# Sums of squares for the weight bounds, 512 and 64 columns down, and products on VectorE in a fused attention and gated block

## The chip, the cores and the metric

The kernel runs on one core of a Trainium2 chip. The metric is the device time of one execution in microseconds (us). Engines are named as the profile names them: PE is TensorE's matmul, PEld its weight load, DVE is VectorE, ACT ScalarE, POOL GpSimd, and SP the engine whose queue issues the DMAs.

## The reference

For x of 2048 rows and 576 columns, normalized to xn (mean and variance over the columns):

```
xn = layernorm(x)
q, k, v = split(xn @ wqkv)                 # 32 heads of 18
s = softmax(q k^T / sqrt(18), causal, window of 256 keys) v, heads joined, @ wo
h = (xn @ w_gate) * (xn @ w_up)            # 4608 hidden columns, no nonlinearity
g = silu(h @ w_down)
out = x + s * g
```

All inputs and the output are float32. Every product of two float32 matrices is made on PE from float16 halves: a high part and a low part, in three passes (high with high, high with low, low with high).

## The kernel before, in words

**Prologue (about 180 us).** The rows are normalized and transposed into `XT`, v is made for all rows and q and k are made and written to DRAM. Meanwhile the first weights and sums for the gated part are prepared at hand-set places.

**Slots.** The gated part works in 72 slots: 18 groups of 256 hidden columns, and in each group four chunks (c0 to c3) of 512 rows. A slot has 16 places. `seven_place` (L1110) issues 96 matmuls of 256 columns in a slot, spread over the places by `SEVEN_N`: seven units `q`, in the order 0, 2, 1, 3, 4, 5, 6, which together make gate and up by a scheme with seven instead of eight block products, from weights (`upw`), sums of weight blocks (`tw`) and sums of x blocks (`sx`). At place 11 `seven_half` (L1066, L1068) adds four matmuls that use 64 rows. A unit's result is read by `seven_copy` (ACT, L1078) or `seven_add` (DVE, L1082) into `gt`, and a following unit accumulates in the same PSUM bank; there are two such `up` banks. `seven_mult` (L1088) multiplies gate by up, 256 columns at a time, into `ht`: four products a slot, those of units 1, 4 and 5 on POOL and that of unit 6 on DVE. `h_hi` (ACT, L968) and `h_lo` (DVE, L973) split `ht` into the halves `hh`.

**Down.** `down` (L986) multiplies a slot's `hh` by the down weights `dnw` in the slot that follows: eight runs of six matmuls of 288 columns (four row blocks, two halves of the 576 columns). Each run fills the single `dn` PSUM bank, and DVE adds it, times a scale, into `acc` in SBUF (L991; L989 in the first group). The last six slots use the four `s` banks instead.

**Attention.** In slots 1 to 64 one step s of attention (two heads, 512 queries) lies in each slot. For each of four query blocks i and two heads j: `score_pairs` (PE, L867, two blocks at a time, 54 rows, the two heads in two row halves of the array), `score` (DVE, L877: adds the mask, takes the maximum, writes `sm_`), `shifted` (ACT, L885), `probs` (ACT: exponential L889, copy to float16 `pp` L892), `turn_probs` (POOL, L898: the low part by a subtraction; after the second head SP issues a DMA that transposes `pp` into `pt`, L901), `weigh` (PE, L910, 37 columns). `finish` (DVE, L921 to L925) divides by the row sums, `finish2` (POOL) splits, and the output goes to DRAM. `load_k`, `load_q`, `load_v` are DMAs for the step that follows.

**Weights.** For each group, one group ahead: `ffn_raw` loads gate, up and down weights (one buffer of each kind); `ffn_amax` (DVE, L410) takes the largest absolute value of each half, six reductions a group; `ffn_spread_out` sends these bounds to DRAM and `ffn_spread_in` loads them into all partitions; `ffn_scale` makes scales that are powers of two; `up_hi`, `t_hi`, `dn_hi` (ACT, L181) and `up_lo`, `t_lo`, `dn_lo` (DVE, L184) split the scaled weights; `t_sum` (POOL, L476) makes the sums of weight blocks; `dn_low` (POOL, L573) makes a third form of the down weights.

**What sets the order.** The program is a list written out by hand: `at(slot, place, f, ...)` puts f at a place (places over 15 run on into the slots that follow), and table `AT` holds the places: for a group counted from the start of the group before it, for a step of attention from the start of its slot. At a place the matmuls of `seven_place` come first, then the list's entries, `score_pairs` ahead of `down` ahead of the rest. Each engine works through its own instructions in that order, and SP its DMAs.

Of the kernel before, what the change touches and what calls it, by code (L numbers as in the profile page):

```python
# [20 lines left out]
def kernel(  # L21
# [46 lines left out]
    AT = {"amax": (13, 16, 22, 24, 6, 10),  # L68
           "dn": ((43, 46), (48, 49), (52, 54)),
           "down": (7, 9, 11, 13, 15, 17, 19, 22),  # L70
           "end": (28, 29, 33),
           "g0": (-21, -19, -13, -18, -14, -12, -11, -9),
           "h": ((16, 18), (18, 21)),
           "load": (0, 12, 12),
           "mult": {1: 2, 4: 1, 5: 1, 6: 0},
# [6 lines left out]
           "pairs": (3, 12),  # L82
           "raw": (6, 8, 13, 15, -3, -3),
           "scale": (25, 31, 38),
           "sum": ((32, 36, 46, 61, 61), (40, 48, 48, 62, 62)),
# [5 lines left out]
           "t_hi": ((57, 58), (62, 62)),  # L91
           "t_lo": ((57, 60), (64, 65)),
           "u0": ((-6, -4, -4, -3), (-5, -2, 4, -3)),
           "up_hi": (40, 44, 61, 69),
           "up_lo": (42, 44, 64, 71)}
# [309 lines left out]
    def ffn_amax(g, kind, half):  # L405
        if (g, "am") not in SC:
            SC[g, "am"] = ring.tile([128, 2, 3], F32, name="am", bufs=2)
        r = RAW[g, kind]
        r = r[:, half] if kind == 2 else r[:, :, half * 128:(half + 1) * 128]
        nc.vector.tensor_reduce(SC[g, "am"][:, half, kind:kind + 1], r, axis=AX.X if kind == 2 else AX.XY,  # L410
                                op=OP.max, apply_absolute_value=True)

    def first_bound(kind):

        if kind == 0:
            SC[0, "am"] = ring.tile([128, 2, 3], F32, name="am", bufs=2)
            nc.gpsimd.memset(SC[0, "am"], 0.0)
        am = SC[0, "am"]
        if kind < 2:
            square(am[:, 0, kind:kind + 1], RAW[0, kind].rearrange("p k n -> p (k n)"),  # L420
                   rv.rearrange("p k n -> p (k n)").bitcast(BF))
        else:
            nc.scalar.activation(am[:, 0, 0:2], am[:, 0, 0:2], AF.Sqrt)

    def ffn_spread_out(g):
        am = SC.pop((g, "am"))
        both = ring.tile([128, 3], F32, name="both", bufs=1)
        nc.vector.tensor_reduce(both, am.rearrange("p h k -> p k h"), axis=AX.X, op=OP.max)
        spread_out(f"f{g}", both, 3)
# [10 lines left out]
    def ffn_scale(g):  # L440
        sc = SC[g] = ring.tile([128, 12], F32, name="sc", bufs=3)
        nc.vector.tensor_reduce(sc[:, 0:3], SC.pop((g, "sp")), axis=AX.X, op=OP.max)
        power(sc[:, 0:3], sc[:, 3:6], sc[:, 6:9], FTOP)
        nc.gpsimd.tensor_tensor(sc[:, 9:10], sc[:, 3:4], sc[:, 4:5], op=OP.mult)
        nc.gpsimd.tensor_scalar(sc[:, 9:10], sc[:, 9:10], C_FFN, None, op0=OP.mult)
        nc.gpsimd.tensor_tensor(sc[:, 9:10], sc[:, 9:10], sc[:, 5:6], op=OP.mult)

    def up_hi(g, k):
        w = UW[g, k] = up_ring()
        hi(w[:, 0:5], RAW[g, k % 2][:, :, k // 2 * 128:k // 2 * 128 + 128], SC[g][:, 6 + k % 2:7 + k % 2])  # L450
# [120 lines left out]
    def dn_low(g, k):  # L571
        w = DW[g, k]
        nc.gpsimd.tensor_scalar(w[:, 2], w[:, 0], 1.0 / LO, None, op0=OP.mult)  # L573
# [32 lines left out]
    for k in range(3):  # L606
        at(0, AT["g0"][k], first_bound, k)
    for half in range(2):
        at(0, AT["g0"][3 + half], ffn_amax, 0, 2, half)
    for k, f in enumerate((ffn_spread_out, ffn_spread_in, ffn_scale)):  # L610
# [216 lines left out]
    QS, KS, VT, SP, SM, PP, PT, PVB, OB, O3, MX = {}, {}, {}, {}, {}, {}, {}, {}, {}, {}, {}  # L827
# [42 lines left out]
    def score(s, j, i):  # L870
        ps = SP.pop((s, j, i))
        n = (i + 3 - max(first_kb(s), i)) * 128
        sm = att.tile([128, 384], F32, name="sm_", bufs=4)
        if j == 0:
            MX[s, i] = att.tile([128, 2, 2], F32, name="mx", bufs=3)
        mx = MX[s, i][:, :, j]
# [403 lines left out]
```

## Time and profile before

| | |
|---|---|
| median of 3 runs | 1661.95 us (1661.13 to 1664.15) |
| the profiled execution | 1662.5 us, of which span (first to last instruction) 1660.8 us |
| granted TensorE clock | 1.0 |
| PE, DVE, ACT, POOL busy | 1599.0, 1387.8, 1029.3, 966.8 us |

The page's row of a group reads: line, engine, operation, what it writes and reads, shape, count, then busy time and the mean of one in ns, then the idle time of the engine ahead of these and what ended it. A row of waits reads: who waited for whom, total us, times, the longest. A row of the windows view gives a stretch, its length, and for each engine the busy time (with the count of instructions), then clock, DMA share and GB/s. In a timeline the first number is the start, the second the duration, and x6 stands for six merged instructions. Busy times count overlapping instructions once; the durations of neighbours on one engine overlap a little, so the distance between starts is the shorter measure of cost.

### The profile page before, as it was taken

Reading aid. Unit: us, or ns where it says so; the run is one execution under the profiler, and the core shown is the slowest. Engines: PE = TensorE matmul, PEld = TensorE weight load, DVE = VectorE, ACT = ScalarE, POOL = GpSimd, SP = SyncE. Lnnn points to the kernel's source line nnn. Section 1 sums busy time; section 2 is a strip of 40 time slices with the busy share of each in tenths; the row PEclk is TensorE's granted clock in tenths of the full one; section 3 lists DMA queues with packets and bytes.
Section 4 is the critical chain, followed back from the end, with each engine's and each line's share of the span. In section 5 each row is a group of like instructions: output and inputs, shape, how many; then the busy total and the mean of one; then the engine's idle time right before and its main releaser. Section 6 shows DMA issues by size and latency. Waiting matters only on the chain.

```text
span 1660.8 us, 40615 instructions
## 1 busy us (share of the span) xinstructions
PE 1599.0 (96%) x15498; PEld 1232.4 (74%) x15498; DVE 1387.8 (84%) x3136; ACT 1029.3 (62%) x1934; POOL 966.8 (58%) x1209
## 2 busy tenths in 40 slices
PE   8999899999999999999999999999999999999999
PEld 5464577877877777777777777777777777778787
DVE  7537789889898989898989898989898989987655
ACT  6434476767676777767776676777767776743230
POOL 3124675757575767676766767676767685843100
PEclk9999999999999999999999999999999999999999
DMA  9562346565656777767677677768776867651228
GB/s 233 164 183 100 111 81 129 94 125 97 124 108 118 136 124 130 124 131 123 136 118 141 119 144 110 146 111 150 108 148 107 153 106 150 118 102 34 63 65 221
DMA packets 565748, 206.95 MB, mean 125 GB/s; under 512 B 506288, under 2 KB 546352, under 8 KB 565552
## 3 DMA queue, kind: packets, MB, share of 16 engines
q1 hardware_dynamic: 565552, 204.35, 63.0%
q8 instruction: 121, 1.98, 0.5%
q14 instruction: 75, 0.61, 0.1%
HBM read 76.63 MB, written 23.75 MB: 60 GB/s over the span
## 4 chain that ended last, share of the span: by engine, by line
PE 59%; DVE 30%; DMA 5%; issue 3%; POOL 1%; ACT 1%; SPq 0%; DVEq 0%; POOLq 0%; ACTq 0%
PE up L1110 25%; PE dn L986 16%; DVE acc L991 5%; DVE gt L1082 4%; DVE upw L184 4%; DVE hh L973 4%; PE s L372 3%; DMA pt<-pp 3%; DVE tw L184 3%; PE pv L910 2%; PE s L986 2%; PE s L1217 2%; DVE ht L1088 2%; PE s L867 1%; PE up L1217 1%
## 5 line engine op out<-in xcount | busy, mean ns | idle before, releaser
L986 PE MATMUL dn<-dnw,hh 128*128 128x288 f16 x3168 | 475.1, 286 | 26.0 <-DVE acc L991 22.1
L986 PEld LDWEIGHTS <-hh 128*128 128x128 f16 x3456 | 328.1, 98 | 150.3 <-issue 81.6
L1110 PEld LDWEIGHTS <-tw 128*128 128x128 f16 x3456 | 317.6, 97 | 63.6 <-issue 23.6
L1110 PEld LDWEIGHTS <-upw 128*128 128x128 f16 x3456 | 327.9, 98 | 45.4 <-DVE gt L1082 1.8
L1110 PE MATMUL up<-XT,upw 128*128 128x256 f16 x2304 | 329.8, 272 | 1.0 <-DVE gt L1082 0.9
L991 DVE SCALAR_TENSOR_TENSOR acc<-dn,sc,acc 128x288 f32<-128x288 f32 x496 | 253.3, 511 | 90.5 <-PE dn L986 87.0
L885 ACT ACTIVATE mx<-mx,sig 128x2 f32<-128x2 f32 x256 | 98.3, 384 | 308.2 <-DVE mx L877 308.0
L1088 POOL TENSOR_TENSOR ht<-gt 128x256 f32<-128x256 f32 x216 | 158.3, 733 | 207.9 <-ACT gt L1078 127.3
L1082 DVE SCALAR_TENSOR_TENSOR gt<-up,gt 128x512 f32<-128x512 f32 x360 | 246.0, 683 | 39.4 <-PE up L1110 22.1
L1110 PE MATMUL up<-XT,tw 128*128 128x256 f16 x1728 | 245.9, 272 | 10.3 <-DVE gt L1082 10.3
L1110 PE MATMUL up<-sx,tw 128*128 128x256 f16 x1728 | 223.6, 272 | 0.3 <-ACT gt L1078 0.3
L910 PEld LDWEIGHTS <-pt 128*128 128x128 f16 x2880 | 118.4, 96 | 20.1 <-DMA pt<-pp 9.9
L910 PE MATMUL pv<-vt,pt 128*128 128x37 f16 x2880 | 123.0, 179 | 6.5 <-DMA pt<-pp 6.4
L973 DVE SCALAR_TENSOR_TENSOR hh<-hh,ht 128x512 f16<-128x512 f16 x144 | 128.5, 893 | 0.0
L1078 ACT ACTIVATE gt<-up 128x512 f32<-128x512 f32 x144 | 84.9, 590 | 63.3 <-PE up L1110 62.0
L1110 PE MATMUL up<-sx,upw 128*128 128x256 f16 x864 | 117.7, 273 | 1.5 <-DVE gt L1082 1.5
L968 ACT ACTIVATE hh<-ht 128x512 f16<-128x512 f32 x144 | 89.3, 620 | 47.0 <-POOL ht L1088 46.9
L184 DVE SCALAR_TENSOR_TENSOR upw<-raw,sc,upw 128x640 f16<-128x640 f32 x72 | 95.6, 1329 | 0.0
L476 POOL TENSOR_TENSOR tf<-raw 128x256 f32<-128x256 f32 x102 | 91.4, 896 | 1.3
L410 DVE TENSOR_REDUCE am<-raw 128x1 f32<-128x640 f32 (+1 forms) x104 | 81.7, 786 | 0.0
L181 ACT ACTIVATE upw<-raw,sc 128x640 f16<-128x640 f32 x72 | 58.7, 817 | 15.6 <-DVE sc L160 10.4
L867 PE MATMUL s<-ks,qs 54*128 54x384 f16 (+2 forms) x512 | 63.7, 317 | 2.9 <-DMA qs<-qk_d 2.7
(2310 smaller groups left out, 2854.6 us busy)
## 6 DMA issues: line engine op xcount, KB each, us to landing
raw<-in_B_w_down_dram SPq DMA_DIRECT2D x36, 288.0 KB
qk_d<-qp SPq DMA_DIRECT2D x18, 512.0 KB
raw<-in_B_w_gate_dram SPq DMA_DIRECT2D x36, 256.0 KB
raw<-in_B_w_up_dram SPq DMA_DIRECT2D x36, 256.0 KB
vt<-v_d SPq DMA_DIRECT2D x48, 111.0 KB
ks<-qk_d SPq DMA_DIRECT2D x96, 54.0 KB
v_d<-vo SPq DMA_DIRECT2D x16, 296.0 KB
xr<-in_A_x_dram SPq DMA_DIRECT2D x16, 288.0 KB
```

The costliest lines, as they stand in the source:

```text
L184: nc.vector.scalar_tensor_tensor(w, rv, s, h, op0=OP.mult, op1=OP.subtract)
L476: nc.gpsimd.tensor_tensor(t[:, to], x0, x1, op=OP.subtract)
L885: nc.scalar.activation(mx[:, 1], mx[:, 0], AF.Identity, bias=sig[:, 2:3], scale=sig[:, 1:2])
L910: nc.tensor.matmul(PVB[s][:, j, i, :VW], pt[:, 2 * nb * j + n], VT[s][:, lo_ + n % nb, j * VW:(j + 1) * VW], start=n == 0, stop=n == 2 * n ...
L968: nc.scalar.activation(hh[:, 0], h, AF.Copy, scale=1.0 / LO)
L973: nc.vector.scalar_tensor_tensor(hh[:, 1], hh[:, 0], -LO, h, op0=OP.mult, op1=OP.add)
L986: nc.tensor.matmul(ps[:, :HALF], a, b, start=q == 0, stop=q == len(l) - 1)
L991: nc.vector.scalar_tensor_tensor(d, ps[:, :HALF], SC[g][:, 9:10], d, op0=OP.mult, op1=OP.add)
L1078: nc.scalar.activation(seven_new(sl, name), CH[q], AF.Copy, scale=H_SC)
L1082: nc.vector.scalar_tensor_tensor(seven_new(sl, name), CH[q], H_SC, x, op0=OP.mult, op1=OP.add)
L1088: eng.tensor_tensor(HT[sl, f][:, 256 * i:256 * i + 256], u[:, 0:256], u[:, 256:512], op=OP.mult)
L1110: nc.tensor.matmul(CH[q][:, o], a, b, start=CH["first"], stop=last and q != 4, skip_group_check=q in ON)
```

## The change

1. **Bounds.** `ffn_amax` is one ACT square with a sum for each kind (128 x 1280 for gate and up, 128 x 1152 for down) instead of two DVE reductions; its output goes to a `upw` buffer that is allocated earlier for it. `ffn_scale` takes a root by halving the exponent (two small DVE operations more); three small POOL operations move to `ffn_scale2` at a later place. The reduction over halves in `ffn_spread_out` goes.
2. **Down.** Four runs of six matmuls of 512 columns, one for each row block, and a fifth run of 24 matmuls of 64 columns that does all four row blocks' last columns in one bank; five DVE evictions of 512, 512, 512, 512 and 256 elements.
3. **Products.** All four of `seven_mult` on DVE, that of unit 4 five places behind its unit.
4. **Second scores** at place 11 instead of 12, right behind the half passes; the first at place 4 instead of 3.
5. **Probabilities.** The two heads share a tile `sm_` (two buffers of 768 instead of four of 384), and after both exponentials one ACT copy of up to 768 elements replaces two; `pp` holds both high parts, then both low parts.
6. **Finish** multiplies by the reciprocal in PSUM (288 elements) ahead of the additions instead of after them (144).
7. **Places.** New values in table `AT`, for the prologue's sums and their engines too. `dn_low`, `finish2` and the subtractions get a switch for another engine that is off.

```diff
-    AT = {"amax": (13, 16, 22, 24, 6, 10),
+    AT = {"amax": (15, 20, 11),
+           "eng": (1, 1, 1, 1, 0, 0, 0, 0, 0, 0, 0, 0, 0, 0),
-           "dn": ((43, 46), (48, 49), (52, 54)),
+           "dn": ((42, 42), (48, 54), (52, 56)),
-           "down": (7, 9, 11, 13, 15, 17, 19, 22),
+           "down": (7, 10, 13, 16, 20),
-           "h": ((16, 18), (18, 21)),
+           "h": ((15, 18), (18, 21)),
-           "load": (0, 12, 12),
+           "load": (0, 8, 10),
-           "mult": {1: 2, 4: 1, 5: 1, 6: 0},
+           "mult": {1: 1, 4: 5, 5: 1, 6: 1},
-           "pairs": (3, 12),
+           "pairs": (4, 11),
-           "raw": (6, 8, 13, 15, -3, -3),
+           "raw": (4, 8, 13, 15, -1, 0),
-           "scale": (25, 31, 38),
+           "scale": (23, 31, 35, 48),
-           "up_hi": (40, 44, 61, 69),
+           "up_hi": (42, 36, 63, 69),
...
-    def ffn_amax(g, kind, half):
...
-        nc.vector.tensor_reduce(SC[g, "am"][:, half, kind:kind + 1], r, axis=AX.X if kind == 2 else AX.XY,
-                                op=OP.max, apply_absolute_value=True)
+    def ffn_amax(g, kind):
...
+        am, r = SC[g, "am"], RAW[g, kind].rearrange("p k n -> p (k n)")
+        to = rv if g == 0 else UW[g, 0]
+        square(am[:, kind:kind + 1], r, to.rearrange("p k n -> p (k n)").bitcast(BF))
...
     def probs(s, j, i):
         sm, mx, n = SM[s, j, i]
         nc.scalar.activation(sm, sm, AF.Exp, bias=mx[:, 1:2], scale=sig[:, 0:1])
-        if j == 0:
+        if j == 1:
             PP[s, i] = att.tile([128, 1536], F16, name="pp", bufs=3)
-        nc.scalar.copy(PP[s, i][:, 2 * n * j:2 * n * j + n], sm)
+            nc.scalar.copy(PP[s, i][:, 0:2 * n].rearrange("p (j n) -> p j n", j=2), SMT.pop((s, i))[:, :, 384 - n:])
...
+        nc.vector.tensor_tensor(pv[:, :, :, 0:2 * DH], pv[:, :, :, 0:2 * DH], rc.to_broadcast([128, 2, 4, 2 * DH]),
+                                op=OP.mult)
...
-        nc.vector.tensor_tensor(o3, o3, rc.to_broadcast([128, 2, 4, DH]), op=OP.mult)
...
     def down(sl, n):
...
+        cols = slice(0, 512) if n < 4 else slice(512, D)
+        for i in (n,) if n < 4 else range(4):
+            to = ps if n < 4 else ps[:, 64 * i:64 * i + 64]
...
+        d, src = acc[:, 4 * c + n, cols] if n < 4 else acc[:, 4 * c:4 * c + 4, cols], ps
+        if n == 4:
+            src = ps[:, 0:256].rearrange("p (i n) -> p i n", i=4)
...
-            at(sl, place + AT["mult"][4], seven_mult, sl, "v", 1, 1, gp)
+            at(sl, place + AT["mult"][4], seven_mult, sl, "v", 1, 1, (gp, vec)[AT["eng"][1]])
```

More of the change, by code (lines that the diff above doesn't have):

```diff
@@ L403, in ffn_raw @@
             nc.sync.dma_start(r[:, part], w_down[g * 256 + part * 128:g * 256 + (part + 1) * 128])
-    def ffn_amax(g, kind, half):
[L406 to L410, printed above, removed]
-                                op=OP.max, apply_absolute_value=True)
[L413 to L423, printed above, removed]
+    def ffn_amax(g, kind):
+        if kind == 2:
+            SC[g, "am"] = ring.tile([128, 3], F32, name="am", bufs=2)
+            if g:
+                UW[g, 0] = up_ring()
+        am, r = SC[g, "am"], RAW[g, kind].rearrange("p k n -> p (k n)")
+        to = rv if g == 0 else UW[g, 0]
+        square(am[:, kind:kind + 1], r, to.rearrange("p k n -> p (k n)").bitcast(BF))
     def ffn_spread_out(g):
[L426 to L429, printed above, removed]
+        spread_out(f"f{g}", SC.pop((g, "am")), 3)
     def ffn_spread_in(g):
@@ L448, in up_hi @@
     def up_hi(g, k):
-        w = UW[g, k] = up_ring()
+        if (g, k) not in UW:
+            UW[g, k] = up_ring()
+        w = UW[g, k]
         hi(w[:, 0:5], RAW[g, k % 2][:, :, k // 2 * 128:k // 2 * 128 + 128], SC[g][:, 6 + k % 2:7 + k % 2])
@@ L606 @@
     for k in range(3):
[L607 to L610, printed above, removed]
+        at(0, AT["g0"][k], ffn_amax, 0, (2, 0, 1)[k])
+    for k, f in enumerate((ffn_spread_out, ffn_spread_in, ffn_scale, ffn_scale2)):
         at(0, AT["g0"][5 + k], f, 0)
@@ L933, in finish2 @@
         oh, ol = (ob[:, k, :, f].rearrange("p i (j d) -> p i j d", j=2) for k in range(2))
-        nc.gpsimd.tensor_copy(oh, ov)
+        if AT["eng"][5]:
+            nc.scalar.copy(oh, ov)
+        else:
+            nc.gpsimd.tensor_copy(oh, ov)
         nc.gpsimd.tensor_tensor(ol, ov, oh, op=OP.subtract)
@@ L1003 @@
                 at(b, max(AT["raw"][2 * kind + part], part if g == 1 else -16), ffn_raw, g, kind, part)
-            for half in range(2):
-                at(b, AT["amax"][2 * kind + half], ffn_amax, g, kind, half)
-        for f, p in zip((ffn_spread_out, ffn_spread_in, ffn_scale), AT["scale"]):
+            at(b, AT["amax"][kind], ffn_amax, g, kind)
+        for f, p in zip((ffn_spread_out, ffn_spread_in, ffn_scale, ffn_scale2), AT["scale"]):
             at(b, p, f, g)
@@ L1021 @@
             at(sl, (17, 18)[ft] if last else AT["h"][1][ft], h_lo, sl, ft)
-        for n in range(8):
-            at(sl + 1, ((6, 7, 8, 9, 10, 11, 13, 15) if last else AT["down"])[n], down, sl, n)
+        for n in range(5):
+            at(sl + 1, ((5, 7, 9, 11, 13) if last else AT["down"])[n], down, sl, n)
     CH = {}
@@ L1131, in seven_read @@
             seven_copy(sl, 1, "11")
[L1132 removed]
+            at(sl, place + AT["mult"][1], seven_mult, sl, "11", 0, 0, (gp, vec)[AT["eng"][0]])
         elif q == 3:
```

60 lines of the change are left out of this document (33 added, 27 removed), and 22 rows, old and new, of the table AT.

## The prediction

> **What bounds the kernel now.** I read the page first, for the engines' shares:
>
> ```profile
> span 1660.8 us, 40615 instructions
> PE 1599.0 (96%) x15498; PEld 1232.4 (74%) x15498; DVE 1387.8 (84%) x3136; ACT 1029.3 (62%) x1934; POOL 966.8 (58%) x1209
> PE 59%; DVE 30%; DMA 5%; issue 3%; POOL 1%; ACT 1%; SPq 0%; DVEq 0%; POOLq 0%; ACTq 0%
> ```
>
> PE looks full, yet 30% of the chain that ended last runs over DVE. So I cut one group of four slots (10) out of the steady part and set a late slot without attention beside it, in the windows view:
>
> ```profile
> core 0: us, PE busy (x) PEld busy (x) DVE busy (x) ACT busy (x) POOL busy (x), PEclk, DMA share, GB/s
> 967.50:988.20 20.70, 19.57 (x205) 15.41 (x204) 20.67 (x44) 14.28 (x27) 12.06 (x16) 1.00 0.80 164
> 988.20:1008.30 20.10, 19.26 (x206) 15.31 (x205) 16.64 (x43) 13.27 (x27) 10.73 (x14) 1.00 0.77 133
> 1008.30:1028.00 19.70, 19.48 (x207) 15.42 (x206) 16.71 (x42) 15.13 (x29) 13.62 (x19) 1.00 0.68 111
> 1028.00:1048.40 20.40, 19.64 (x207) 15.48 (x205) 18.93 (x41) 14.50 (x28) 19.18 (x21) 1.00 0.65 107
> 1539.30:1556.10 16.80, 16.80 (x151) 14.14 (x149) 11.57 (x22) 2.34 (x4) 2.38 (x4) 1.00 0.02 1
> 179.90:199.50 19.60, 11.83 (x102) 9.42 (x101) 17.23 (x23) 6.16 (x11) 17.71 (x16) 1.00 0.42 123
> 253.90:483.60 229.70, 225.48 (x2306) 181.00 (x2304) 203.58 (x499) 156.43 (x318) 146.84 (x202) 1.00 0.59 110
> 562.60:1450.00 887.40, 856.28 (x8979) 677.43 (x8977) 803.16 (x1827) 629.11 (x1167) 611.33 (x738) 1.00 0.72 129
> ```
>
> I call the four slots of a group c0 to c3. In c0 DVE is busy 20.67 of 20.70 us: it is the bound. In c3 it has 1.47 us free, while POOL is busy 19.18 of 20.40. In c1 and c2 DVE has 3 us free. The last row holds 44 slots, 20.17 us each, 80.7 a group.
>
> What would PE alone need? Its timeline in c2 gives the start of each run of matmuls:
>
> ```profile
> 1019.25 0.90 PE L986 MATMUL dn<-dnw,hh 128*128 128x288 f16 x6
> 1019.98 0.93 PE L1110 MATMUL up<-sx,tw 128*128 128x256 f16 x7
> 1020.74 0.38 PE L1110 MATMUL up<-XT,upw 128*128 128x256 f16 x2
> 1021.06 0.28 PE L1066 MATMUL up<-XT,upw 64*128 64x256 f16 x1
> ...
> 1021.18 0.27 PE L1066 MATMUL up<-XT,upw 64*128 64x256 f16 x1
> ...
> 1021.38 0.91 PE L986 MATMUL dn<-dnw,hh 128*128 128x288 f16 x6
> 1022.13 0.46 PE L910 MATMUL pv<-vt,pt 128*128 128x37 f16 x12
> 1022.43 0.93 PE L1110 MATMUL up<-XT,tw 128*128 128x256 f16 x7
> 1023.29 0.50 PE L867 MATMUL s<-ks,qs 54*128 54x384 f16 x4
> 1023.72 0.72 PE L1110 MATMUL up<-XT,tw 128*128 128x256 f16 x5
> ```
>
> From start to start, six down matmuls of 288 columns take 0.73 us (0.122 each, 0.42 ns a column) and seven of 256 take 0.76 (0.109 each). Two of 256 ahead of the half passes take 0.32, 0.10 more than 0.22: going from 128 to 64 rows costs 0.10. The second pair of half passes needs 0.20 where the first needed 0.12: 0.08 to go back. The scores, in 54 rows, show the same: 0.86 for seven ahead of them (0.10 over), 0.43 for two pairs of 384 columns at 0.16 (0.11 over). A slot has three such excursions. PE's floor is the late slot's 16.80, two score excursions (0.52 each with the way in) and 48 pv matmuls at 0.025: 19.0 us. What lies above it, 1.1 us a slot, is waiting.
>
> **The change, part by part.** Durations by operation, from the groups:
>
> ```profile
> L991 DVE SCALAR_TENSOR_TENSOR acc<-dn,sc,acc 128x288 f32<-128x288 f32 x496 | 253.3, 511 | 90.5 <-PE dn L986 87.0
> L1088 POOL TENSOR_TENSOR ht<-gt 128x256 f32<-128x256 f32 x216 | 158.3, 733 | 207.9 <-ACT gt L1078 127.3 <-DVE gt L1082 80.3
> L1088 DVE TENSOR_TENSOR ht<-gt 128x256 f32<-128x256 f32 x72 | 52.2, 726 | 0.0
> L410 DVE TENSOR_REDUCE am<-raw 128x1 f32<-128x640 f32 x68 | 55.1, 810 | 0.0
> L300 ACT ACTIVATE rv<-raw 128x1280 bf16<-128x1280 f32 x2 | 2.6, 1278 | 1.9 <-POOL am L417 1.9
> L892 ACT CAST pp<-sm__2242 x1: 511/511/511, 214.4 to 214.4; 128x384 f16<-128x384 f32 x1
> L898 POOL TENSOR_TENSOR pp<-sm__2242,pp x1: 924/924/924, 215.0 to 215.0; 128x384 f16<-128x384 f32 x1
> ```
>
> *Scores behind the half passes.* The second score excursion joins that of the half passes: one way in and one way out go, 0.19 us a slot.
>
> *Down by 512 and 64 columns.* 48 matmuls of 0.122 are 5.86 us. After: 24 of 512 columns at 0.42 ns (0.217) and 24 of 64 at 0.027, 5.86 again. The cover is that a weight load hides behind matmuls even of 37 columns: twelve pv took 0.30 us, loads included. I take 0. On DVE eight evictions become five. DVE's timeline, here at the start of c0, shows what instructions cost from start to start:
>
> ```profile
> 967.54 0.68 DVE L1082 SCALAR_TENSOR_TENSOR gt<-up,gt 128x512 f32<-128x512 f32 x1
> 968.14 0.50 DVE L991 SCALAR_TENSOR_TENSOR acc<-dn,sc,acc 128x288 f32<-128x288 f32 x1
> 968.57 0.89 DVE L1088 TENSOR_TENSOR ht<-gt 128x256 f32<-128x256 f32 x1
> 969.38 1.53 DVE L184 SCALAR_TENSOR_TENSOR upw<-raw,sc,upw 128x640 f16<-128x640 f32 x1
> 970.84 0.74 DVE L184 SCALAR_TENSOR_TENSOR tw<-tf,sc,tw 128x512 f16<-128x512 f32 x1
> 971.50 0.51 DVE L991 SCALAR_TENSOR_TENSOR acc<-dn,sc,acc 128x288 f32<-128x288 f32 x1
> ```
>
> An eviction of 288 takes 0.43. One of 512 lies between 0.60 (L1082) and 0.66 (L184, which like it takes its scale from a column): 0.66. Of 256: about 0.40. So 4 x 0.66 + 0.40 = 3.04 for 3.44: -0.40 a slot. PE's one down bank is asked for every third place or later, not every second: an eviction may come about a place (1.2 us) later before PE feels it.
>
> *Bounds on ACT.* DVE loses, at 0.07 less than the duration (0.81 for 640 elements; by the elements 0.73 for the down weights' 576), 2 x 0.66 + 0.74 = 2.06 us in c0 and 3 x 0.74 = 2.2 in c1. ACT gains two squares of 1.28 and one near 1.2, 3.7 us a group, and gives back four of eight 0.51 copies a slot for a wider one: a copy of 768 lies between 0.51 and 1.02; with 0.17 us for 224 elements more (L991 to L1082 on DVE, 0.51 to 0.68) I take 0.83, -0.7 us a slot. ACT has 5 us a slot free; a square can hold one gt copy back by 1.3 us, and q1, which waits for it, comes only after q2. I take 0, up to 0.5 a group. Two small DVE operations on three columns more and one fewer, and `ffn_scale2` later on POOL: 0. The scale itself moves from place 38 to 35, the load of the spread bounds stays at 31: if DVE stood for all three places it cost 3.6 us a group; since the q and v loads no longer stand right ahead of that load on SP, I take 0 to 0.5.
>
> *Three products to DVE.* This is the term that decides. On DVE the product depends on what POOL does. Two rows, of late slots with little POOL work and of c3; c0 had 0.89, above:
>
> ```profile
> L1088 DVE TENSOR_TENSOR ht<-gt 128x256 f32<-128x256 f32 x3 | 1.2, 416 | 0.0
> L1088 DVE TENSOR_TENSOR ht<-gt 128x256 f32<-128x256 f32 x1 | 1.2, 1184 | 0.0
> ```
>
> Bounds 0.34 and 1.10 us from start to start. The mean, 0.726, gives 0.65; POOL loses three products (2.2 us) a slot, so it collides less: 0.62, three times 1.86 us a slot. The same relief of DVE's other operations with two SBUF inputs (0 to -0.4) I leave out. [...]
>
> *Finish* multiplies 288 elements in PSUM instead of 144 in SBUF: between -0.4 (the one that goes has two SBUF inputs and can collide like a product) and +0.43 (an eviction of 288, were the old one free) a slot; nearer to neither, I take 0.
>
> *The sum.* DVE, start to start: c0 20.67 - 0.40 - 2.06 + 1.86 = 20.07; c1 15.9; c2 18.17; c3 18.93 - 0.40 + 1.86 = 20.39. PE's floor is now 18.85. So c1 and c2 go to PE: 19.05 and 19.2 with small waits. c3 and c0, back to back, are DVE's: 40.46, 0.5 for the waits of its own that stay, less the 1.2 that PE now bears: 39.75. The group is 78.0 after 80.7, and 0.5 goes to new stalls (below): -2.2, 12 groups, -26 us. The twelve earlier slots (229.7 us, shorter scores, 19.14 each): 0.19 and some 0.3 of waits, -6. The prologue's reordered steps end in the first slot, 179.90 to 199.50, where PE is busy 11.83 of 19.60 us and DVE and POOL work off the sums: three bounds go and three products come there, so I take 0, with up to 7.8 to win and as much to lose. The other first slots -1; the end, where DVE has 5 us a slot free, 0. Together -33 us: the profiled execution took 1662.5 (span 1660.8, 1.7 around it), 0.5 over the median, so 1629.
>
> **Rivals.** PE's waits in the steady 44 slots:
>
> ```profile
> PE dn L986 <- DVE acc L991: 17.3, 43, 1.1
> PE pv L910 <- DMA pt<-pp: 6.4, 9, 1.2
> ```
>
> *DVE's lateness never reaches PE.* For it: the down bank, most of the waits, gets slack. All slots near 18.95: 48 x 1.2 + 12 x 0.7 = -66, some 1597.
>
> *The products are dear.* At 0.9 us each, c0 and c3 gain 0.84 again, c2 0.5: the 2.2 are eaten, and 1655 stays. For it: the products of c0 and c3 shown above. Against: those products stood where POOL had a subtraction each time. From about 0.95 on there is no gain; at 1.10 it is 1670.
>
> *Transposes come too late (slower).* Before, the first copy and subtraction (L892, L898) lay ahead of or beside the second exponential; now two exponentials, one copy and both subtractions follow each other ahead of a transpose: 0.83 for 2 x 0.51, and one subtraction of 0.92 more, 0.7 us later, 256 times. Besides, four q loads and the v load move on SP from place 12 to 8 and 10, past the transposes of places 9 and 12, which stand behind them if SP is late. Against: pv waited for a transpose 9 times in 44 slots, so most have slack; the up weights' loads, which follow the transpose of place 12, get out sooner, and so does the next transpose; POOL is freer. It decides from one transpose in six late in full (43 x 0.75 = 32); with one in three it is 1692.
>
> *The 64-column matmuls wait for their weights (slower).* A load's own row:
>
> ```profile
> L986 PEld LDWEIGHTS <-hh 128*128 128x128 f16 x3456 | 328.1, 98 | 150.3 <-issue 81.6 <-DVE hh L973 0.6
> ```
>
> At 0.098 a pair instead of 0.027, 24 x 0.07 x 72 = +122: 1751. The pv rows, 0.025 a pair, speak against it. [...]
>
> **How the numbers follow.** The forecast, 1629 (1612 to 1648), has 0.55; PE's floor (1597) 0.12; dear products (1650 to 1670) 0.18, of which 0.08 faster, 0.05 within 0.2%, 0.05 slower; late transposes 0.12; weights 0.03. Measurement tells 0.2%, 3.3 us. So faster 0.75, same 0.05, slower 0.20. The range 1600 to 1664 leaves out the two slower mechanisms and part of the floor case.
>
> **What would show it.** Right: c0 and c3 shorten to about 19.9, c1 and c2 to about 19.1; PE's waits for L991's successor fall below 10 us; the DVE product's mean is 0.6 to 0.7; the half passes run straight into scores; down of 64 at 0.027. Wrong: a product mean above 0.9 with c3 over 20.7; PE waiting on pt<-pp over 30 us; 64-column pairs near 0.1; DVE waiting for the spread bounds, whose use moves from seven to four places behind their load.

## The result, and the profile after

The changed kernel takes 1653.93 us (median of 20 runs, 1647.09 to 1662.78), the kernel before on the same chips 1663.34 (20 runs, 1658.35 to 1668.92). The ratio is 0.9944, 95% interval 0.9929 to 0.9959: 9.4 us less, where 33 were forecast. The profiled execution after took 1657.39 us, 3.5 over its median; the readings below are its own, against the 1660.8 us span of before.

The page: the span, the engines' shares and the chain that ended last.

```profile
span 1655.5 us, 40444 instructions
PE 1584.0 (96%) x15498; PEld 1122.7 (68%) x15498; DVE 1353.2 (82%) x3049; ACT 1042.3 (63%) x1781; POOL 784.0 (47%) x993
PE 56%; DVE 23%; DMA 8%; issue 4%; SPq 4%; POOL 3%; ACT 1%; DVEq 0%; ACTq 0%; POOLq 0%
```

DVE's part of the chain fell from 30% to 23%, but DMA and SP's queue, together 5% before, now hold 12%. Something that DMAs set has come into the path. Where it sits shows in the windows view of the changed kernel: the same group (10) as before, slot by slot, then slot 70, the twelve early slots, and the same 44 steady slots that the prediction cut out.

```profile
958.80:978.00 19.20, 19.02 (x207) 13.89 (x206) 18.42 (x44) 16.20 (x28) 9.85 (x13) 1.00 0.87 163
978.00:998.50 20.50, 19.02 (x206) 13.80 (x204) 14.20 (x37) 14.31 (x25) 7.91 (x10) 1.00 0.93 141
998.50:1019.00 20.50, 19.19 (x206) 13.79 (x205) 18.21 (x43) 14.79 (x25) 11.90 (x15) 1.00 0.64 121
1019.00:1038.30 19.30, 19.07 (x207) 13.92 (x206) 18.97 (x41) 12.55 (x22) 15.36 (x18) 1.00 0.55 109
1546.30:1570.70 24.40, 18.69 (x151) 13.09 (x149) 13.50 (x26) 5.33 (x9) 0.19 (x1) 0.86 0.43 100
251.30:485.20 233.90, 224.78 (x2307) 163.05 (x2305) 200.58 (x484) 157.65 (x289) 116.07 (x166) 0.99 0.59 108
562.00:1439.60 877.60, 842.46 (x8978) 610.02 (x8977) 771.08 (x1772) 635.61 (x1057) 497.16 (x606) 1.00 0.75 130
```

The DVE-bound slots c0 and c3 went down, to 19.20 and 19.30, and DVE is no longer full in c0. But c1 and c2, which had DVE to spare, went up, to 20.50. The 44 steady slots gained 9.8 us (887.4 to 877.6), the early ones lost 4.2 (229.7 to 233.9), and slot 70 takes 24.40 us for the work of a late slot that the prediction set at 16.80.

Over all runs of this study the same figure, the mean slot of the twelve steady groups (slots 16 to 63, worked out from the start of each slot's first up matmul), tells most:

| kernel | c0 | c1 | c2 | c3 | group | slot 70 |
|---|---|---|---|---|---|---|
| before | 20.73 | 19.76 | 19.62 | 20.41 | 80.5 | 20.8 |
| after | 19.13 | 20.62 | 20.57 | 19.23 | 79.5 | 24.4 |
| up loads later | 19.14 | 18.94 | 21.34 | 19.23 | 78.7 | 25.8 |
| two copies | 20.24 | 19.08 | 19.99 | 19.18 | 78.5 | 25.1 |
| scale alone at 38 | 19.17 | 20.17 | 21.84 | 19.24 | 80.4 | 24.7 |
| scale and its POOL part at 35 | 19.10 | 20.28 | 19.84 | 18.90 | 78.1 | 24.9 |
| the same at 38 | 19.07 | 20.17 | 19.85 | 18.88 | 78.0 | 25.3 |
| products on POOL | 21.30 | 20.99 | 20.63 | 19.17 | 82.1 | 24.0 |
| before, down by 512 | 20.00 | 21.27 | 19.41 | 19.78 | 80.5 | 23.0 |
| the same, up loads later | 20.07 | 19.53 | 19.71 | 19.74 | 79.1 | 22.5 |
| loads, scale and wo_scale | 19.22 | 19.05 | 20.81 | 18.87 | 78.0 | 16.8 |
| copies, scale and wo_scale | 20.25 | 19.36 | 19.17 | 19.00 | 77.8 | 16.8 |
| loads, copies, scale and wo_scale | 20.33 | 18.87 | 20.64 | 18.88 | 78.7 | 16.8 |
| wo_scale alone later | 19.18 | 20.61 | 20.62 | 19.23 | 79.6 | 16.8 |

Who waits on PE now? Its largest waits after:

```profile
PE pv L908 <- DMA pt<-pp: 24.1, 20, 2.6
PE up L1116 <- DVE gt L1088: 11.8, 7, 5.7
PE dn L991 <- DVE acc L998: 10.6, 25, 0.9
PE dn L991 <- DVE hh L975: 9.5, 12, 0.8
```

The wait that the change was to relieve, for the down bank, halved (10.6 us after, 22.1 in the whole span before). The one for transposes went from 6.4 to 24.1 us.

**The place in c1.** SP's timeline of the changed kernel around the start of c1 (978.0), and then PE's row at the place that waits:

```profile
978.84 0.78 SPq L177 DMA_DIRECT2D raw<-in_B_w_up_dram  x1
...
980.86 0.48 SPq L179 DMA_DIRECT2D raw<-in_B_w_up_dram  x1
981.51 1.96 SPq L899 DMA_TRANSPOSE pt<-pp  x1
```

```profile
987.25 0.47 PE L908 MATMUL pv<-vt,pt 128*128 128x37 f16 x12 [1.48 <-DMA pt<-pp]
```

The third transpose of the step stands on SP behind four issues of raw up weights (2.5 us). It goes out 3.5 us into c1. PE goes on 5.7 us later, after standing for 1.48. Over the twelve steady groups this transpose goes out 4.1 us into c1 (the median of the SP rows), where before it was 3.3.

**The place in c2.** DVE's timeline after, at place 35, where `ffn_scale` now lies, shows three of its small dependent operations; then POOL's shows what ran beside them.

```profile
1004.53 0.77 DVE L433 TENSOR_SCALAR sc<-sc 128x3 f32<-128x3 f32 x1
1005.33 0.84 DVE L157 TENSOR_SCALAR sc<-sc 128x3 f32<-128x3 f32 x1
1006.20 0.65 DVE L159 TENSOR_SCALAR sc<-sc 128x3 int32<-128x3 int32 x1
```

```profile
1004.35 1.79 POOL L896 TENSOR_TENSOR pp<-sm__15722,pp 128x384 f16<-128x384 f32 x2 [2.76 <-ACT pp L890]
1006.11 0.72 POOL L472 TENSOR_TENSOR tf<-raw 128x256 f32<-128x256 f32 x1
```

Three columns took 0.65 to 0.84 us an operation, where each of the same kind took 0.17 before (L156, L158 and L160, 0.169 to 0.172 in all 18 groups). The whole chain lasts 3.9 us, and the eviction and `hh` behind it come late: in this slot PE waits 0.51 for L998 and 0.80 for L975. Before, POOL did not run there, because it stood at the scale's own POOL part, right behind; POOL's waits before have this row:

```profile
POOL sc L444 <- DVE sc L158: 68.2, 18, 8.5
```

**The clock.** The windows view after, cut at the clock's steps: a stretch of 3.4 us with a wait in it, and the one that follows it; then another wait, after which the clock stayed.

```profile
258.20:261.60 3.40, 1.50 (x24) 1.13 (x23) 2.59 (x11) 2.85 (x8) 0.79 (x1) 1.00 0.49 124
261.60:265.00 3.40, 3.40 (x13) 1.50 (x11) 0.42 (x1) 3.13 (x6) 1.98 (x4) 0.50 1.13 224
...
1224.20:1227.60 3.40, 1.71 (x23) 1.38 (x24) 1.38 (x5) 3.37 (x7) 0.00 (x0) 1.00 0.60 94
```

PE at a granted clock of 0.50 does 13 matmuls in 3.4 us, six of them of 512 columns at 0.43 us instead of 0.215. After has 24.0 us of half clock in all, 3.5 of them in the tail; before has 3.3, all in the tail. So some 20 us ran at half speed: at most about 10 us lost, an estimate that takes PE as the bound in all of it.

### The profile page after: what moved, and what is told of

It reads as the page before. It is cut to its first block, busy times and chain, and to the rows that moved or that the text cites. A ratio compares the mean times of both kernels' runs of the same rounds, so it can differ in the third digit from the quotient of the medians.

```text
span 1655.5 us, 40444 instructions
## 1 busy us (share of the span) xinstructions
PE 1584.0 (96%) x15498; PEld 1122.7 (68%) x15498; DVE 1353.2 (82%) x3049; ACT 1042.3 (63%) x1781; POOL 784.0 (47%) x993
## 4 chain that ended last, share of the span: by engine, by line
PE 56%; DVE 23%; DMA 8%; issue 4%; SPq 4%; POOL 3%; ACT 1%; DVEq 0%; ACTq 0%; POOLq 0%
PE up L1116 23%; PE dn L991 14%; DMA pt<-pp 6%; PE s L373 3%; DVE gt L1088 3%; PE pv L908 3%; DVE acc L998 3%; DVE ht L1094 2%; DVE upw L185 2%; PE s L991 2%; DVE hh L975 2%; PE s L1223 2%; PE s L864 1%; PE up L1223 1%; PE up L373 1%
## 5 line engine op out<-in xcount | busy, mean ns | idle before, releaser
L991 PE MATMUL dn<-dnw,hh 128*128 128x512 f16 (+1 forms) x3168 | 448.9, 287 | 21.4 <-DVE acc L998 10.6
L1116 PEld LDWEIGHTS <-tw 128*128 128x128 f16 x3456 | 329.5, 98 | 78.0 <-issue 13.3
L991 PEld LDWEIGHTS <-hh 128*128 128x128 f16 x3456 | 224.6, 98 | 198.8 <-issue 37.6
L998 DVE SCALAR_TENSOR_TENSOR acc<-dn,sc,acc 128x512 f32<-128x512 f32 x310 | 214.7, 693 | 115.5 <-PE dn L991 110.2
L908 PE MATMUL pv<-vt,pt 128*128 128x37 f16 x2880 | 123.8, 179 | 24.3 <-DMA pt<-pp 24.1
L1094 DVE TENSOR_TENSOR ht<-gt 128x256 f32<-128x256 f32 x288 | 147.0, 530 | 0.0
L975 DVE SCALAR_TENSOR_TENSOR hh<-hh,ht 128x512 f16<-128x512 f16 x144 | 102.4, 711 | 0.1
L472 POOL TENSOR_TENSOR tf<-raw 128x256 f32<-128x256 f32 x102 | 74.2, 735 | 6.9 <-DVE sc L430 6.8
L301 ACT ACTIVATE upw<-raw 128x1280 bf16<-128x1280 f32 (+1 forms) x51 | 62.7, 1230 | 14.4 <-DMA raw<-in_B_w_up_dram 14.1
L185 DVE SCALAR_TENSOR_TENSOR upw<-raw,sc,upw 128x640 f16<-128x640 f32 x72 | 69.7, 969 | 0.0
L472 POOL TENSOR_TENSOR tf<-raw,tf 128x256 f32<-128x256 f32 x68 | 49.7, 731 | 35.3 <-DVE tw L185 35.3
```

The costliest lines, as they stand in the source:

```text
L185: nc.vector.scalar_tensor_tensor(w, rv, s, h, op0=OP.mult, op1=OP.subtract)
L472: nc.gpsimd.tensor_tensor(t[:, to], x0, x1, op=OP.subtract)
L908: nc.tensor.matmul(PVB[s][:, j, i, :VW], pt[:, nb * j + n + n // nb * nb], VT[s][:, lo_ + n % nb, j * VW:(j + 1) * VW], start=n == 0, stop ...
L975: nc.vector.scalar_tensor_tensor(hh[:, 1], hh[:, 0], -LO, h, op0=OP.mult, op1=OP.add)
L991: nc.tensor.matmul(to, a, b, start=q == 0, stop=q == len(l) - 1)
L998: nc.vector.scalar_tensor_tensor(d, src, SC[g][:, 9:10], d, op0=OP.mult, op1=OP.add)
```

## The experiments

Unless it is said otherwise, each kernel is the changed one with the edit shown. Times are medians, ratios are to the kernel before.

### The transposes of c1: loads later, and the two copies back

```diff
-    AT = {"amax": (15, 20, 11),
+    AT = {"amax": (15, 25, 11),
-           "raw": (4, 8, 13, 15, -1, 0),
-           "scale": (23, 31, 35, 48),
+           "raw": (4, 8, 17, 17, -1, 0),
+           "scale": (27, 31, 35, 48),
```

> The changed kernel with the loads of the up weights moved from places 13 and 15 to 17, behind the transpose of place 16 on SP (their bound from 20 to 25, its way out from 23 to 27). Theory A: c1 stands (20.6 us on average, with 0.8 to 2.6 us of waiting at place 6) because the third transpose of a step leaves SP behind four weight loads, and its data behind theirs: then c1 falls to about 19.0 and the time by 15 to 20 us, to about 1636. Rival B: the transpose is late because of the joint copy and the two subtractions ahead of it; then SP would only have waited for POOL, c1 stays near 20.3 and the time within 4 us of the changed kernel's 1654.

Measured: 1649.3 us, ratio 0.9916 (0.989 to 0.9943). c1 went from 20.62 to 18.94, the whole loss of c1 and more: with the loads out of its way the transpose comes in time. But c2 rose from 20.57 to 21.34 and took half of it back, and the time fell by only some 5 us where 15 to 20 were expected. The edit also sends the bounds out four places later, which bears on c2 (below).

```diff
-            SMT[s, i] = att.tile([128, 2, 384], F32, name="sm_", bufs=2)
-        sm = SMT[s, i][:, j]
+        sm = att.tile([128, 384], F32, name="sm_", bufs=4)
...
-        if j == 1:
+        if j == 0:
             PP[s, i] = att.tile([128, 1536], F16, name="pp", bufs=3)
-            nc.scalar.copy(PP[s, i][:, 0:2 * n].rearrange("p (j n) -> p j n", j=2), SMT.pop((s, i))[:, :, 384 - n:])
+        nc.scalar.copy(PP[s, i][:, n * j:n * j + n], sm)
```

> The changed kernel with two copies of 384 and four score tiles as before, the rest as changed. If the joint copy and the later subtraction make the third transpose late (rival B of the first run), the wait in c1 shrinks by about 0.7 us a group, in all 10 us, less what ACT's 0.8 us a slot more costs. If SP and the loads make it late (theory A), the wait stays and the time is the changed kernel's or up to 5 us above.

Measured: 1638.92 us, ratio 0.9843 (0.9814 to 0.9872), 15 us better than the change as a whole. c1 is at 19.08: starting the first copy and subtraction earlier also brings the transpose in time. It still stands behind the four loads, but goes out 3.0 us into c1 instead of 4.1 (medians). So the loads and the joint copy make it late together, and either repair is enough; neither theory had that. It costs c0 1.1 us (19.13 to 20.24), where POOL's subtractions now lie beside DVE's work: the rows of `hh`, `ht` and `upw` there add up to 1.7 us more.

### The scale in c2

```diff
-           "scale": (23, 31, 35, 48),
+           "scale": (23, 31, 38, 48),
-           "up_hi": (42, 36, 63, 69),
+           "up_hi": (42, 39, 63, 69),
```

> The changed kernel with the weights' scale back at place 38 (first use from 36 to 39). Theory A: at place 35 four small DVE operations of it, three of them 0.65 to 0.84 us long instead of 0.17, lie in POOL's subtractions and hold the evictions and the scores up, so that PE loses 1.6 us in every c2; at 38 POOL has a pause: c2 goes from 20.5 to about 19.2 and the time falls by 15 to 20 us. Rival B: c2 is late because of the three products on DVE, and the scale only stands where the lateness shows: c2 stays over 20 and the time within 5 us.

Measured: 1674.35 us, ratio 1.0061 (1.0043 to 1.0078). The expectation fell: moving the scale back to its old place makes it worse, with c2 at 21.84. It is not the place. What differs from before is `ffn_scale2`, which keeps POOL from running on. So the next two runs put it back behind the scale, at either place:

```diff
-           "scale": (23, 31, 35, 48),
+           "scale": (23, 31, 35, 35),
```

> The changed kernel with the three small POOL operations of ffn_scale2 at place 35, right behind the scale, as they stood before. Theory C: in the kernel before POOL stood at these operations until DVE had finished the scale (68 us of POOL waits in all, 18 times), and so did not collide with it; since they moved to 48 POOL goes on and each small DVE operation waits out a POOL operation. At 35 the third subtractions still lie beside the first half of the scale, so c2 falls from 20.6 to between 19.3 and 20.0, 8 to 15 us. Rival: the chain of seven dependent DVE operations is itself too long for the place; c2 and the time stay within 4 us of the changed kernel's 1654.

```diff
-           "scale": (23, 31, 35, 48),
+           "scale": (23, 31, 38, 38),
-           "up_hi": (42, 36, 63, 69),
+           "up_hi": (42, 39, 63, 69),
```

> The kernel with the scale at place 38 (c2 21.8 us, 1674 us) with ffn_scale2 also at 38 instead of 48. Theory C: POOL now waits for the scale as in the kernel before, the small operations take 0.17 instead of 0.6 to 0.8 us, and c2 falls from 21.8 to about 19.3: 25 to 30 us below the kernel with 38 and 48, about 1645. Rival: the place of POOL's operations does not matter, c2 stays over 21 and the time within 5 us of 1674.

Measured: 1632.83 us, ratio 0.9814 (0.9797 to 0.983), and 1633.27, ratio 0.9831 (0.9789 to 0.9872). Three POOL operations of 0.2 us, moved by some places, are worth 21 us of the changed kernel and 41 at place 38. The groups view (count, busy, mean in ns) of the scale at 38 without `ffn_scale2` behind it:

```profile
L159 DVE TENSOR_SCALAR sc<-sc 128x3 int32<-128x3 int32 x18 | 11.8, 653 | 0.6
L157 DVE TENSOR_SCALAR sc<-sc 128x3 f32<-128x3 f32 x18 | 11.7, 649 | 0.6
```

and with it:

```profile
L157 DVE TENSOR_SCALAR sc<-sc 128x3 f32<-128x3 f32 x18 | 3.5, 197 | 0.6
L159 DVE TENSOR_SCALAR sc<-sc 128x3 int32<-128x3 int32 x18 | 3.1, 170 | 0.6
```

POOL, which must wait for L159, leaves DVE alone until then. L157, L159 and the L161 that follows get shorter by 1.25 us together; c2 by 2.0, and the half clock falls from 34.2 to 12.8 us. Both gains are larger than expected (8 to 15 us, and 25 to 30), though c2 stopped at 19.84 and 19.85: with both parts at 35 the twelve steady groups take 17 us less, 9 of them in c2 and 4 each in c1 and c3.

### The scale of wo in slot 70

```diff
-        at(NSLOT - 2, 3 * k + 2, wo_split, k)
+        at(NSLOT - 2, 3 * k + 10, wo_split, k)
...
-    at(NSLOT - 2, 0, wo_scale)
+    at(NSLOT - 2, 9, wo_scale)
```

> The changed kernel with the scale of the output weights at place 9 of slot 70 instead of 0 (its splits 8 places later). Theory A: DVE stands there for a DMA that spreads the bound, PE stands 5.9 us behind it and runs 6.8 us more at half its clock; 9 places later the DMA has landed: slot 70 goes from 24.4 to about 17, and the time falls by 6 to 8 us. Rival: the wait only moves with it, time within 2 us.

Measured: 1649.72 us, ratio 0.99 (0.9866 to 0.9935), some 4 us under the changed kernel by the medians, less than the 6 to 8 expected, and the times of the two kernels overlap. Slot 70 of the profiles says it more sharply, 24.38 to 16.84. Two rows of the changed kernel's timelines, DVE's and PE's, then the window of slot 70 with the edit:

```profile
1553.97 0.29 DVE L1188 TENSOR_REDUCE ps_o<-spread 128x1 f32<-128x128 f32 x1 [5.00 <-DMA spread<-sd_wo]
```

```profile
1558.52 2.08 PE L1116 MATMUL up<-XT,tw 128*128 128x256 f16 x9 [5.71 <-DVE gt L1088]
```

```profile
1548.00:1564.80 16.80, 16.80 (x151) 12.44 (x149) 11.19 (x23) 3.46 (x6) 0.19 (x1) 1.00 0.76 146
```

DVE stood 5.00 us at a transfer that had just been issued, with PE's own work behind it. The kernel before waited there too (5.31 us); its PE stood 3.82 and met no half clock, after's stood 5.71 and then had 6.8 us of it.

### Single terms: the products, and down alone

```diff
-           "eng": (1, 1, 1, 1, 0, 0, 0, 0, 0, 0, 0, 0, 0, 0),
+           "eng": (0, 0, 0, 1, 0, 0, 0, 0, 0, 0, 0, 0, 0, 0),
-           "mult": {1: 1, 4: 5, 5: 1, 6: 1},
+           "mult": {1: 2, 4: 1, 5: 1, 6: 0},
```

> The changed kernel with three products back on POOL and at their places before. If the products on DVE are what DVE pays for the change (the prediction's dear rival), c2 and c3 get shorter and the time falls. By the trace a product costs 0.53 us on DVE on average, and POOL, freed of 2.2 us a slot, collides less: then the slots c0 and c3 go back up by 0.5 to 1.5 us each and the time rises by 10 to 30 us.

Measured: 1681.94 us, ratio 1.0103 (1.0064 to 1.0141), 28 us above the changed kernel. The three products on DVE are a gain; the groups of this run show what leaving them on POOL does to the one that is on DVE either way, 0.887 us where all four on DVE have a mean of 0.530:

```profile
L1094 DVE TENSOR_TENSOR ht<-gt 128x256 f32<-128x256 f32 x72 | 63.8, 887 | 1.8
```

The loss lies in c0 (19.13 to 21.30) and less in c1; in c3 it makes no difference.

The second of this kind is the kernel before with the down product alone by 512 and 64 columns (new `down`, as in the diff of the change):

```diff
-           "down": (7, 9, 11, 13, 15, 17, 19, 22),
+           "down": (7, 10, 13, 16, 20),
```

> The kernel before with one part of the change alone: down by 512 and 64 columns at the places 7, 10, 13, 16, 20. The forecast's terms: PE's time for down as before (5.9 us a slot), DVE 0.4 us a slot less, and one down bank asked for every third place. If that is right c0 and c3, where PE waited for DVE's evictions, gain 0.5 to 1 us each and the others a little: 12 to 25 us below the kernel before. If the single bank, now held 1.3 us by PE and 0.75 by DVE, is the tighter chain, no gain or a loss of up to 10 us.

Measured: 1658.94 us, ratio 0.9961 (0.9948 to 0.9974): about 6 us, less than expected. c0 and c3 gained 0.7 and 0.6, and c1 lost 1.5. PE's waits in this run begin with

```profile
PE pv L910 <- DMA pt<-pp: 25.5, 19, 3.0
PE up L1114 <- DVE gt L1086: 12.5, 16, 4.3
```

The wait for the down bank is gone from the list, and the wait for transposes has come up to what the whole change shows. Attention's steps here are those of before: it is not the new order of exponentials and copies that makes the transposes late, or not it alone. The last of this kind puts the loads later in that kernel:

```diff
-    AT = {"amax": (13, 16, 22, 24, 6, 10),
+    AT = {"amax": (13, 16, 25, 26, 6, 10),
-           "raw": (6, 8, 13, 15, -3, -3),
-           "scale": (25, 31, 38),
+           "raw": (6, 8, 17, 17, -3, -3),
+           "scale": (27, 31, 38),
```

> The kernel before with the down product by 512 and 64 columns, and the second up weights' raw loads at place 17 instead of 13 and 15 (bound at 25 and 26, spread at 27). Theory A (down alone won only 5.5 us because c1 then waits for its third transpose, which stands on SP behind these loads: c1 19.76 to 21.27, and the waits for transposes 6.4 to 25.5 us): c1 falls to 19.6 or less and the time to 1640 us (1632 to 1646). Rival B (c1 lost by something else, DVE or the half clock): c1 stays above 20.7 and the time at 1655 us or more.

Measured: 1642.76 us, ratio 0.9871 (0.9857 to 0.9885), c1 at 19.53. Most of what down was worth had been taken back by one transpose behind four loads.

### Versions put together

> Three repairs at once: the second up weights' raw loads at place 17 instead of 13 and 15 (with their bound at 25 and the spread at 27), the scale and its POOL part both at 35, wo_scale at place 9 of slot 70. Theory A (three separate losses: the third transpose in c1, the bare DVE chain in c2, the scale's wait in slot 70): the gains add up. From 1632.8 us with the scale part alone, 12 x 1.3 us of c1 and 7.5 us of slot 70 go: 1610 us (1605 to 1616); c1 under 19.2, c2 under 20.0, slot 70 under 17. Rival B (what one repair gives in c1, the later bounds and scale take back in c2, as the later loads alone raised c2 from 20.57 to 21.34): c2 stays above 20.5 and the time is 1620 us or more.

Measured: 1625.41 us, ratio 0.9768 (0.9745 to 0.979). The gains do not add up: c1 is at 19.05, but c2 at 20.81; both numbers of rival B are met. The wait has moved on to c2's third transpose. SP's timeline of this run:

```profile
985.00 0.33 SPq L425 DMA_DIRECT2D tf<-sd_f  x1
...
986.33 4.36 SPq L899 DMA_TRANSPOSE pt<-pp  x1
```

It goes out behind the load that spreads the bounds to all partitions and stays 4.36 us at the head of SP's queue. In the twelve steady cases of this run with that load just ahead the mean is 3.80 us, in the other 180 it is 1.70 (worked out from their rows); the changed kernel with the later loads alone has 3.75. That load as a neighbour is not enough to explain it: in the kernel before a transpose stands right behind it too, and the mean is 1.53. What differs is the store that the load reads. With the later loads it goes out 3.1 to 4.6 us ahead of the load, in the kernel before 5.3 to 8.1, in the changed kernel 8.8 to 11.1, where the mean is 2.09. A load that must wait for its store, and holds the transpose behind it, would fit these rows; it was not tried.

> The scale and its POOL part both at 35, wo_scale at place 9, and the probabilities' copies as two of 384 right behind each exponential (as before the change) instead of one of 768. Theory A (the two copies let the third transpose start sooner in c1, but put POOL's subtractions beside DVE's work in c0): c1 19.1, c0 20.2, c2 at most 19.9; 1632.8 less 7.5 (slot 70) and no net gain from the copies: 1625 us (1618 to 1632). Rival B (subtractions do not cost c0 anything once the scale is repaired): c0 19.2 and 1612 us or less.

Measured: 1618.17 us, ratio 0.9716 (0.97 to 0.9731), the best of this study, at the lower edge of what theory A gave. c0 pays as expected (20.25), c1 and c2 are at 19.36 and 19.17. Its slots 40 to 42 in the windows view, and its wait for transposes:

```profile
944.50:964.90 20.40, 19.31 (x207) 13.86 (x205) 20.20 (x44) 16.96 (x32) 10.70 (x14) 1.00 0.86 158
964.90:983.90 19.00, 19.00 (x206) 13.82 (x204) 15.20 (x37) 15.12 (x29) 8.07 (x11) 1.00 0.98 140
983.90:1003.00 19.10, 19.02 (x206) 13.81 (x204) 17.33 (x42) 15.57 (x29) 12.05 (x19) 1.00 0.75 136
```

```profile
PE pv L907 <- DMA pt<-pp: 9.5, 10, 2.3
```

In c1 and c2 PE is idle for under 0.1 us in all; only c0 is DVE's, busy 20.20 of 20.40.

> The three repairs of the run before last and the two copies as well. Theory A (the later loads have already freed the third transpose, so the two copies have nothing left to win in c1 and cost 1.1 us in c0): 8 to 14 us above the three repairs without them. Rival B (transposes are late in other slots too, and two copies win there): at or below the three repairs alone.

Measured: 1633.87 us, ratio 0.9827 (0.9797 to 0.9857). With the copies in, the later loads cost 15.7 us: c2 rises from 19.17 to 20.64. The numbers of theory A are met (8.5 above the three repairs), but its reason only in half: c0 does pay, and the edit that frees c1 burdens c2. The transposes behind the bounds' load take 3.39 us here, after 3.75 and 3.80 in the other two changed kernels with this edit, and c2 is over 20.6 in all three.

## Why the prediction was wrong in size

The sign and the range (1600 to 1664) held; the time came out 25 us above the forecast, with 9.4 of the 33 us. What failed are three terms that the sum had at nothing or next to it: new stalls at 0.5 us a group, `ffn_scale2` later on POOL at 0, and the end at 0. c1 and c2 came out 2.9 us a group over the forecast, c0 and c3 1.4 under it. None of the prediction's signs of being wrong showed it: PE's wait for transposes is 24.1 us, not over 30, and a product has 0.530. It was c1 and c2, which were to come to about 19.1, that told. By the prediction's own steps:

**Down: PE 0, DVE -0.40 a slot.** Right for PE, nearly so for DVE. The timeline after gives 1.29 us for six of 512 columns (the next matmul starts at 1012.73; 0.215 each) and 0.71 for 24 of 64 columns:

```profile
1011.44 1.46 PE L991 MATMUL dn<-dnw,hh 128*128 128x512 f16 x6
```

```profile
1024.42 0.87 PE L991 MATMUL dn<-dnw,hh 128*128 128x64 f16 x24
1025.13 0.31 PE L908 MATMUL pv<-vt,pt 128*128 128x37 f16 x6
```

That is 0.030 a pair of 64 columns: the rival in which these wait for their weights (0.098) did not come. On DVE an eviction of 512 lasts 0.747 us (its row is among the groups below) and one of 256 0.474; less the prediction's 0.07 each, five take 3.11 us for its 3.04, so DVE saves 0.33 a slot.

**Half passes and scores, -0.19.** Right by the rows. The second pair of half passes takes 0.11 us, with no way back, and the scores follow at once:

```profile
1013.60 0.27 PE L1072 MATMUL up<-XT,upw 64*128 64x256 f16 x1
1013.71 0.49 PE L864 MATMUL s<-ks,qs 54*128 54x384 f16 x4
```

This and the bounds on ACT were not run by themselves. PE's floor of 18.85 is borne out too: c3 with the scale repaired takes 18.87 to 18.90 us.

**The products at 0.62, and the relief of DVE's other operations, "0 to -0.4", left out.** Both too dear. The groups after:

```profile
L1094 DVE TENSOR_TENSOR ht<-gt 128x256 f32<-128x256 f32 x288 | 147.0, 530 | 0.0
L975 DVE SCALAR_TENSOR_TENSOR hh<-hh,ht 128x512 f16<-128x512 f16 x144 | 102.4, 711 | 0.1
L185 DVE SCALAR_TENSOR_TENSOR upw<-raw,sc,upw 128x640 f16<-128x640 f32 x72 | 69.7, 969 | 0.0
L185 DVE SCALAR_TENSOR_TENSOR tw<-tf,sc,tw 128x512 f16<-128x512 f32 x68 | 50.4, 743 | 0.0
L998 DVE SCALAR_TENSOR_TENSOR acc<-dn,sc,acc 128x512 f32<-128x512 f32 x248 | 185.4, 747 | 98.8 <-PE dn L991 93.4
L920 DVE TENSOR_TENSOR pv<-pv,rc 128x288 f32<-128x288 f32 x64 | 29.8, 466 | 2.2
```

and of the same operations before:

```profile
L973 DVE SCALAR_TENSOR_TENSOR hh<-hh,ht 128x512 f16<-128x512 f16 x144 | 128.5, 893 | 0.0
L184 DVE SCALAR_TENSOR_TENSOR upw<-raw,sc,upw 128x640 f16<-128x640 f32 x72 | 95.6, 1329 | 0.0
L184 DVE SCALAR_TENSOR_TENSOR tw<-tf,sc,tw 128x512 f16<-128x512 f32 x68 | 65.8, 968 | 0.0
```

A product has a mean of 0.530 us, some 0.46 from start to start: 0.16 less than taken, 0.5 a slot for three. The `hh`, `upw` and `tw` operations lost 26.1, 25.9 and 15.4 us, 0.9 a slot, where nothing was counted. The operations with two SBUF inputs, which the prediction had in mind, spread in the trace of before: `upw` 0.872 to 1.534 us, `tw` 0.739 to 1.352, `hh` 0.676 to 1.403 and finish's product (L925) 0.307 to 0.866, 0.307 to 0.309 in the 24 cases with no POOL work beside it; the eviction L991, which reads PSUM, took 0.499 to 0.520. Only part of the 0.9 is shown to be the relief that the prediction named: with the three products back on POOL `tw` is at 0.999 us again, but `hh` at 0.749 and `upw` at 0.931. What shortened these two was not run apart. So the two slots that DVE bounds came out better than forecast: c0 and c3 together 38.4 us after, forecast 39.75. Finish was taken at 0 and is nearly 0 (the multiplication takes 0.466 us, as before).

**"Transposes come too late", a rival at 0.12.** This failed first. It was priced as a case apart, one late transpose in six or none; what came is a milder form of it, 20 waits for 256 transposes, inside the forecast's own case. By the waits it is 17.7 us more for pv, and by the two runs with later loads it is c1's whole loss. The step that failed is "0.5 goes to new stalls" a group: c1 alone came out 1.6 us over its 19.05. The prediction did name the raw up loads, but as a reason against: they "get out sooner, and so does the next transpose". In the steady groups that transpose went out later, 4.1 us into c1 for 3.3 before, behind these loads and behind the joint copy. That the down part by itself, in the kernel before, brings the same wait (25.5 us) points to the link that was left out: once the down bank no longer holds PE, it gets to the transpose earlier.

**"`ffn_scale2` later on POOL: 0".** The dearest step. It was costed by its own work on POOL, 0.6 us, and not by who had been kept quiet by it. With it back behind the scale, 21 us return. The prediction's argument was there, that what POOL does sets how long a DVE operation takes (the product, 0.416 to 1.184 us in before), but applied to operations with two SBUF inputs only. The `tensor_scalar` of this chain have one, and took 0.17 in before and, as medians, 0.43 (L161), 0.65 (L159), 0.77 (L433) and 0.84 (L157) in after, beside POOL's work. The reciprocal in the same chain, of the same three columns, kept its 0.178 us beside POOL.

**"The end 0".** Wrong by 3.6 us in slot 70. A stall of 5 us in DVE stood in the trace of before; the prediction went by the 5 us a slot that DVE had free there on the average.

**What no step had: the clock.** A wait of 1.90 us, at 258.6, had 3.41 us at half clock behind it, as above: up to 1.7 us more, an estimate (half of 3.41) that takes PE as the bound.

Together, of the profiled spans: forecast -33; measured -5.3, of which steady groups -11.9 (12 x 0.99) for -26, early slots +4.2 for -6, slot 70 +3.6 for 0, and -1.2 for the rest. Of the early slots' +4.2, c2 and c3 hold 3.0, which is gone with the POOL part of the scale back at 35; 1.2 is in their c0, where the half clock at 261.6 lies. With the scale repaired and the two copies back the group is 77.8, and the forecast's was 78.0. That these agree so closely is luck, since c0 is dearer there by the copies and DVE's work cheaper than forecast; but it shows that a gain of the size forecast was there, and that the new waits ate most of it.

## What to carry to other kernels

When a wait is removed, look up, for each DMA that the waiting engine meets next, when it is issued and what stands ahead of it on its queue: the gain can end where that slack does. An instruction that makes an engine wait may shelter another engine (here L159 took 0.170 us with `ffn_scale2` behind the scale at 38, 0.653 without); before moving it, see what the first will run in its place and whether the two get in each other's way. And a stall of two microseconds on PE is not worth two microseconds when the clock takes the next 3.4 at half speed, as it did here at 261.6.

## What the runs showed of the hardware that was not expected

- **Half clock after a wait of 1.90 us.** In the trace of after, half clock starts at 186.48, 261.58, 592.67, 1387.97 and 1555.23 us (and in the tail) and lasts 3.413 us, at 1555.23 6.827; the distances of the starts are 22, 97, 233 and 49 times 3.413 us. Cut into stretches of that length, in step with these starts, the trace has PE busy for 0.22 to 1.51 us in the stretches at full clock that half clock follows (1.51 in the one with the wait of 1.90, at 258.6), and for 1.66 or more in all the others (1.66 in the one with a wait of 1.83, at 1224.1). In before, in step with its only half clock, at 1659.54, it is 1.24 ahead of that and 1.47 or more in the others: at about 1.5 it went either way. A wait of 2.62 us (at 1304.5), which fell over two stretches with PE busy for 1.84 and 2.36, had no half clock behind it, nor had the 3.82 us in slot 70 of the kernel before (1.51 and 1.50). So in these two traces the half clock went with little work within a stretch, not with a long wait; why was not tried.
- **Three columns took up to 0.84 us.** A DVE `tensor_scalar` of the scale took 0.17 us in before, where POOL stood, and 0.43 to 0.84 us (medians) in after, beside POOL's work of that place, a reciprocal 0.178 us either way: in this chain the collision, not the size, set the time.
- **A transpose behind the load that spreads the bounds** took 3.75, 3.80 and 3.39 us at SP's head (the means) in the three changed kernels with the later loads; the first that follows this load took 1.53 in the kernel before and 2.09 in the changed kernel. The store that the load reads went out 3.1 to 4.6 us ahead of it in the run of 3.80, 5.3 to 8.1 in before and 8.8 to 11.1 in after; the cause stays open.
